# Spectra: both products copied whole out of PSUM by ScalarE, and VectorE's complex products fed from SBUF alone

## The chip, the cores and the metric

The kernel runs on one core of a Trainium2 chip. The metric is the device time of one execution in microseconds (us); smaller is better. The core's engines work side by side, each through its own queue in order: TensorE (PE, with its weight loads PEld), VectorE (DVE), ScalarE (ACT), GpSimd (POOL), and SyncE (SP), which issues most of the DMAs. TensorE writes its products into PSUM; DVE and ACT read them there; SBUF is the large memory that all engines and the DMAs share.

## The reference

Two independent layers read two inputs of 2048 rows and 576 columns, and their outputs are put side by side:

```python
qkv = (x @ wqkv) ...                          # 32 heads of 18 columns
scores = einsum("bhqd,bhkd->bhqk", q, k) * (Dh ** -0.5)
mask = (i - j >= 0) & (i - j < 256)           # sliding window
a = softmax(where(mask, scores, -1e9)) @ v, heads joined, @ wo

P = exp(dt * A * l)                           # 576 channels, 128 states, l = 0..2047
K = einsum("dn,dnl,dn->dl", C, P, dt * B).real
Kf = rfft(pad(K)); Uf = rfft(pad(u))          # length 4096
y = irfft(Uf * Kf)[:, :2048] + u * Dskip
out = concatenate([a, y])
```

The change touches only `Uf * Kf`: the spectrum of the input times the spectrum of the filter, a complex product for each frequency and channel.

## The kernel before

The work is written as some twenty streams (Python generators), each of which yields at every step. A string of letters, `PLAN`, says in which order the steps are issued: a letter alone takes the next step of a stream, a letter with a digit runs the oldest follow-up that the stream posted under that digit. So the order on every engine is written out by hand and does not depend on how long anything takes.

The part that matters is the last one (`"rest"`). There run together: `smax` (letter s; for a head group and 64 queries at a time it multiplies Q with K, line 831, adds the mask, line 839, and DVE takes the row maximum, line 865, `red`), `scores` (a; the same products once more with the maximum taken off, lines 901 and 914, then ACT takes the exponential into `P`, line 919), `pv` (v; `P` times `V`, line 939, into the PSUM tile `po`), `norm` (n; two DVE transposes, lines 964 and 968, then a POOL multiplication, line 973, an ACT copy, line 977, and a POOL subtraction, line 981), `wo` (w; the last projection) and the convolution: `cspec` (c), `cinv` (d) and `clast` (e).

`cspec` calls `spectra(n)` for 24 tiles, 3 groups of 192 channels by 8 groups of frequencies. For each tile it takes two PSUM slots `pi[0]` and `pi[1]`; a second-stage Fourier matrix is multiplied with a tile `x` that holds 192 columns of the input and 192 of the filter side by side (line 671, 32 matmuls). So `pi[0]` holds the real parts of both spectra and `pi[1]` the imaginary parts, each as 128 partitions x 2 x 384: columns 0 to 191 the input, 192 to 383 the filter. Three follow-ups form the complex product: `first` (c1, ACT, line 679), `second` (c2, DVE, line 686) and `third` (c3, POOL, lines 691 and 692).

All these products go through one PSUM pool, `ring`, of three slots; only `po` has its own. A slot can be written again when the last instruction that reads it is done, so each matmul group waits for the reader of an earlier one. `X`, `t1` and `t2` live in the pool `fy`, with one buffer each.

Of the kernel before, what the change touches and what calls it, by code (L numbers as in the profile page):

```python
# [10 lines left out]
F32 = mybir.dt.float32  # L11
# [3 lines left out]
AF = mybir.ActivationFunctionType  # L15
OP = mybir.AluOpType
# [114 lines left out]
class Kernel:  # L131
# [14 lines left out]
    def pow2_scale(self, parts, nm):  # L146
# [4 lines left out]
        r = sp.tile([128, 1], F32, name=nm + "r")  # L151
        nc.vector.tensor_reduce(m, parts, axis=AX.X, op=OP.max)
        nc.gpsimd.partition_all_reduce(g, m, 128, bass.bass_isa.ReduceOp.max)
# [508 lines left out]
    def spectra(self, n):  # L662
        nc, tt, fy, t = self.nc, self.nc.vector.tensor_tensor, self.p["fy"], n % 8
        x, pi = self.cl.pop(n), (self.slot(), self.slot())
        for i in range(2):
            for q in range(2):
                for s in range(2):
                    for r in range(2):
                        b = 2 * q + (r ^ s)
                        o = (2 * s + q) * 64 + 32 * i  # L670
                        nc.tensor.matmul(pi[i][32 * b:32 * b + 32, s, :384], self.w2[64 * r:64 * r + 64, t, o:o + 32],  # L671
                                         x[64 * r:64 * r + 64, 2 * s + q].rearrange("p m j -> p (m j)"),
                                         start=True, stop=True, skip_group_check=True)
        sh = [128, 2, 2, 192]

        def first():
            X = fy.tile(sh, F32, name="X")
            for i in range(2):
                nc.scalar.activation(X[:, :, i], pi[i][:, :, :192], AF.Copy)  # L679
            self.post("2", (X, *pi), lambda: second(X))  # L680

        def second(X):
            t1 = fy.tile(sh, F32, name="t1")
            t2 = fy.tile(sh, F32, name="t2")
            for i, tm in enumerate((t1, t2)):
                tt(tm, X, pi[i][:, :, 192:384].unsqueeze(2).to_broadcast(sh), op=OP.mult)  # L686
            self.post("3", (t1, t2), lambda: third(t1, t2))

        def third(t1, t2):
            Y = self.Y[n] = self.p["fs"].tile(sh, F32, name="Y")  # L690
            nc.gpsimd.tensor_tensor(Y[:, 0], t1[:, :, 0], t2[:, :, 1], op=OP.subtract)  # L691
            nc.gpsimd.tensor_tensor(Y[:, 1], t1[:, :, 1], t2[:, :, 0], op=OP.add)
            self.n["Y"] += 1
        self.post("1", pi, first)

    def inverse(self, n):
# [167 lines left out]
    def red(self, out, x):  # L864
        self.nc.vector.tensor_reduce(out, x, axis=AX.X, op=OP.max)  # L865
        self.n["max"] += 1
# [319 lines left out]
```

## Time and profile before

| | |
|---|---|
| time, median of 3 runs | 879.57 us (873.76 to 879.66) |
| the profiled execution's own time | 875.76 us |
| its span, first to last instruction | 874.0 us, mean granted TensorE clock 0.923 |
| busy over the span | PE 719.8, DVE 601.3, ACT 526.9, POOL 378.1 us |
| `spectra`, first and last product on DVE | start at 449.6 and 783.9 us |

An execution's time is a little longer than its span, by 1.76 us here. In the groups of instructions a row gives line, engine, operation, output and input with their shapes, the count, then the busy time with the mean of one in ns, and behind the second bar the idle time of the engine just before these instructions and what ended it. In the timeline a row gives start, duration, engine, line, operation, count, and in brackets how long the engine had been idle and who released it; rows with x2 merge two instructions that follow each other.

### The profile page before, as it was taken

The page shows a single profiled execution, that of the slowest core. Times are in us where ns is not written, and L with a number is a line of the kernel's source. Part 1 is how long each engine was busy: PE and PEld are TensorE (multiplying, and loading weights), DVE is VectorE, ACT ScalarE, POOL GpSimd, SP SyncE. Part 2 cuts the span into 40 slices and gives each one's busy share as a digit, 9 for nine tenths or more (in the row PEclk, how much of TensorE's full clock was granted, in tenths as well). Part 3 has the DMA queues.
Part 4 walks back from the last instruction along what each step waited for, and adds up shares of the span by engine and source line. Part 5 has one row for each costly group of instructions (what it writes and reads, how often), then busy time and mean ns, then how long its engine had stood idle before and what let it go on. Part 6 is the DMA issues. An engine that isn't in the chain of part 4 may idle for free. (4 is left out here: it accounts for less than half of the span.)

```text
span 874.0 us, 29447 instructions
## 1 busy us (share of the span) xinstructions
PE 719.8 (82%) x12954; PEld 417.3 (48%) x12954; DVE 601.3 (69%) x798; ACT 526.9 (60%) x709; POOL 378.1 (43%) x295
## 2 busy tenths in 40 slices
PE   3575957999889888896887779868998988989977
PEld 2331523456345644564534445435454544557655
DVE  5865887887987787776757798667787778751010
ACT  3247676578777766672455567646776776666421
POOL 2266857666687755565013424321242151432020
PEclk9985969999999999995889999969999998999998
DMA  9795261546347754569457856947658675746743
GB/s 306 263 236 138 61 162 34 143 92 164 85 103 193 151 131 135 116 158 251 102 184 237 270 182 211 215 116 243 176 156 270 192 238 159 205 128 188 244 139 123
DMA packets 211040, 150.74 MB, mean 172 GB/s; under 512 B 102698, under 2 KB 191530, under 8 KB 210656
## 3 DMA queue, kind: packets, MB, share of 16 engines
q1 hardware_dynamic: 208896, 144.87, 59.0%
q0 software_dynamic: 2016, 3.99, 1.4%
q8 instruction: 101, 1.65, 0.8%
q14 instruction: 27, 0.22, 0.1%
HBM read 83.57 MB, written 65.11 MB: 170 GB/s over the span
## 5 line engine op out<-in xcount | busy, mean ns | idle before, releaser
L865 DVE TENSOR_REDUCE m<-ring 128x2 f32<-128x640 f32 (+4 forms) x256 | 186.8, 779 | 52.8 <-PE ring L839 49.5
L919 ACT ACTIVATE P<-ring,esc 128x1024 f32<-128x1024 f32 (+2 forms) x160 | 167.5, 1060 | 85.6 <-PE ring L914 78.0
L546 POOL TENSOR_TENSOR m<-A,tr 128x1024 f32<-128x1024 f32 x72 | 144.0, 2019 | 77.8 <-DVE m L552 66.7
L939 PE MATMUL po<-P,V 64*32 64x320 f32 (+4 forms) x2816 | 101.6, 364 | 4.7 <-issue 4.7
L831 PE MATMUL ring<-K,Q 54*64 54x320 f16 (+4 forms) x1024 | 82.2, 319 | 26.8 <-DMA K<-kz 8.0
L691 POOL TENSOR_TENSOR Y<-t,t 128x384 f32<-128x384 f32 x24 | 24.0, 1002 | 138.9 <-DVE t L686 129.9
L973 POOL TENSOR_TENSOR osb<-osb,T 128x1024 f32<-128x1024 f32 x16 | 37.9, 2366 | 99.1 <-DVE T L968 61.4
L901 PE MATMUL ring<-Q,K 55*64 55x320 f16 (+4 forms) x1408 | 67.2, 269 | 14.5 <-DVE t L686 5.6
L831 PEld LDWEIGHTS <-Q 54*64 54x64 f16 x1024 | 44.2, 109 | 71.5 <-issue 64.0
L981 POOL TENSOR_TENSOR oh<-osb,oh 128x1024 f16<-128x1024 f32 x16 | 34.1, 2134 | 68.6 <-ACT oh L977 68.5
L178 PE MATMUL pp<-xh,wh 128*128 128x512 f16 x180 | 48.4, 400 | 18.6 <-ACT vst L365 9.2
L686 DVE TENSOR_TENSOR t<-X,ring 128x768 f32<-128x768 f32 x48 | 43.4, 945 | 25.5 <-ACT X L679 18.3
L178 PEld LDWEIGHTS <-wh 128*128 128x128 f16 x324 | 32.0, 102 | 57.7 <-issue 19.4
L901 PEld LDWEIGHTS <-K 55*64 55x64 f16 x1408 | 34.0, 109 | 47.5 <-issue 40.5
L552 DVE TENSOR_TENSOR m<-m,m 128x1024 f32<-128x1024 f32 x36 | 53.4, 1482 | 4.8 <-POOL m L546 4.7
L839 PE MATMUL ring<-sm,idb 64*64 64x128 bf16 x896 | 56.0, 225 | 0.1
L575 PE MATMUL ring<-Q,m 128*32 128x64 f32 x2304 | 42.6, 231 | 16.1 <-DVE m L552 13.4
L939 PEld LDWEIGHTS po<-P,V 64*32 64x32 f32 x2816 | 38.6, 107 | 34.6 <-issue 24.9
L575 PEld LDWEIGHTS ring<-Q,m 128*32 128x32 f32 x2304 | 37.0, 117 | 29.6 <-issue 11.9
L178 PE MATMUL pp<-xh,wl 128*128 128x512 f16 x180 | 50.6, 417 | 0.0
L964 DVE STREAM_TRANSPOSE T<-osb 128x1024 f32<-128x1024 f32 x16 | 19.8, 1235 | 42.1 <-ACT osb L949 42.1
L527 POOL TENSOR_TENSOR tr<-tr,mab 128x768 f32<-128x768 f32 x18 | 33.7, 1871 | 31.2 <-ACT tr L522 31.1
(159 smaller groups left out, 1539.4 us busy)
## 6 DMA issues: line engine op xcount, KB each, us to landing
gx<-ust SPq DMA_DIRECT2D x16, 576.0 KB
gk<-kst SPq DMA_DIRECT2D x18, 512.0 KB
xk<-gx SPq DMA_DIRECT2D x24, 384.0 KB
xk<-gk SPq DMA_DIRECT2D x24, 384.0 KB
h<-ho SPq DMA_DIRECT2D x48, 192.0 KB
hp<-h SPq DMA_DIRECT2D x12, 768.0 KB
Q<-qz SPq DMA_DIRECT2D x16, 512.0 KB
K<-kz SPq DMA_DIRECT2D x16, 512.0 KB
```

What stands on the lines that cost most here:

```text
L178: self.nc.tensor.matmul(ps, u, v, start=(i == 0), stop=(i == len(ops) - 1))
L546: tt(m[part], A[:, ch, a0:a0 + 8].unsqueeze(3).to_broadcast(sh), tr[:, ch, part, 0:8].unsqueeze(2).to_broadcast(sh), op=OP.mult)
L552: self.nc.vector.tensor_tensor(m[0], m[0], m[1], op=OP.add)
L575: nc.tensor.matmul(kp[32 * st:32 * st + 32, j, :], m[:, ch, 32 * term:32 * term + 32], Q[:, ch, term, :], start=(term == 0), stop=(term == ...
L686: tt(tm, X, pi[i][:, :, 192:384].unsqueeze(2).to_broadcast(sh), op=OP.mult)
L831: nc.tensor.matmul(ps[z:z + 64, b, :n], d["Q"][rr, 2 * b + pp, 64 * qb:64 * qb + 64], d["K"][rr, 2 * b + pp, k0:k1], start=True, stop=Fals ...
L839: nc.tensor.matmul(out, self.idb[rr], self.sm[rr], start=False, stop=True, skip_group_check=True)
L865: self.nc.vector.tensor_reduce(out, x, axis=AX.X, op=OP.max)
L901: nc.tensor.matmul(ps[z:z + 64, b, off:off + w], d["K"][rr, 2 * b + pp, kc:kc + 64], d["Q"][rr, 2 * b + pp, q0:q0 + w], start=(k == 0), st ...
L919: nc.scalar.activation(P[:, :, lo:hi], ps[:, :, lo:hi], AF.Exp, scale=self.esc)
L939: nc.tensor.matmul(po[32 * p:32 * p + 32, z, q0:q0 + w], V[64 * z:64 * z + 64, kb * 76 + 19 * p:kb * 76 + 19 * p + 32], P[p % 2][64 * z:64 ...
L973: nc.gpsimd.tensor_tensor(osb, osb, rb, op=OP.mult)
```

## The change

ACT now copies all 384 columns of each slot, both the input's and the filter's, so `X` doubles from 3 KB to 6 KB in each partition (its layout is now part, half of the frequencies, column). DVE's two products take both operands out of `X`, the input's part through a rearranged view so that `t1` and `t2` come out as before, and no longer read PSUM. `post("2", ...)` names only `X`.

```diff
         def first():
-            X = fy.tile(sh, F32, name="X")
+            X = fy.tile([128, 2, 2, 384], F32, name="X")
             for i in range(2):
-                nc.scalar.activation(X[:, :, i], pi[i][:, :, :192], AF.Copy)
-            self.post("2", (X, *pi), lambda: second(X))
+                nc.scalar.activation(X[:, i], pi[i][:, :, :384], AF.Copy)
+            self.post("2", (X,), lambda: second(X))
 
         def second(X):
             t1 = fy.tile(sh, F32, name="t1")
             t2 = fy.tile(sh, F32, name="t2")
             for i, tm in enumerate((t1, t2)):
-                tt(tm, X, pi[i][:, :, 192:384].unsqueeze(2).to_broadcast(sh), op=OP.mult)
+                tt(tm, X[:, :, :, :192].rearrange("p i s j -> p s i j"),
+                   X[:, i, :, 192:].unsqueeze(2).to_broadcast(sh), op=OP.mult)
             self.post("3", (t1, t2), lambda: third(t1, t2))
```

No instruction changes its place on any engine; what changes is what some of them wait for. Behind line 679 the new file has one line more, so line 901 there is 902, 914 is 915, 939 is 940 and 865 is 866 (lines up to 686 keep their numbers). The order on PE at one `spectra` tile, the sixteenth, which starts at 664 us in the trace; its second slot's matmuls come first, then two score blocks, each of which takes the next slot of `ring`. Before:

```order
L671 MATMUL ring<-xk,w_5121 32x384 [waits Activation_49]
L671 MATMUL ring<-xk,w_5121 32x384 x7
L901 LDWEIGHTS K_4393
L901 MATMUL ring<-Q_4392,K_4393 64x320 [waits DVE_49]
...
L914 MATMUL ring<-tm,idb 64x2x128
L901 LDWEIGHTS K_4393
L901 MATMUL ring<-Q_4392,K_4393 64x320 [waits DVE_49]
...
L939 MATMUL po<-P,V_4394 32x320 x8
```

And now:

```order
L671 MATMUL ring<-xk,w_5121 32x384 [waits Activation_49]
L671 MATMUL ring<-xk,w_5121 32x384 x7
L902 LDWEIGHTS K_4393
L902 MATMUL ring<-Q_4392,K_4393 64x320 [waits DVE_49]
...
L915 MATMUL ring<-tm,idb 64x2x128
L902 LDWEIGHTS K_4393
L902 MATMUL ring<-Q_4392,K_4393 64x320 [waits Activation_49]
...
L940 MATMUL po<-P,V_4394 32x320 x8
```

The first block writes the third slot, which an earlier row maximum has to release, in both. The second block writes the slot of `pi[0]`: before it waited for DVE's product, now it waits for ACT's copy. The same tile on DVE, ahead of it the end of one run of row maxima and behind it the next. Before:

```order
L865 TENSOR_REDUCE m<-ring 128x2 [waits PE_49] x10
L686 TENSOR_TENSOR t_10125<-X,ring 128x768 [waits DVE_49,Activation_49,Pool_49]
L686 TENSOR_TENSOR t_10126<-X,ring 128x768 [waits DVE_49,PE_49]
L865 TENSOR_REDUCE m<-ring 128x2 [waits PE_49] x6
L851 TENSOR_SCALAR m_10302<-ring 32x128 [waits DMAHW2_49,DMAHW1_49,DMAHW3_49,DMAHW0_49,PE_49]
```

And now:

```order
L866 TENSOR_REDUCE m<-ring 128x2 [waits PE_49] x10
L686 TENSOR_TENSOR t_10125<-X 128x768 [waits DVE_49,Activation_49,Pool_49]
L686 TENSOR_TENSOR t_10126<-X 128x768 [waits DVE_49]
L866 TENSOR_REDUCE m<-ring 128x2 [waits PE_49] x6
L852 TENSOR_SCALAR m_10302<-ring 32x128 [waits DMAHW2_49,DMAHW1_49,DMAHW3_49,DMAHW0_49,PE_49]
```

The two products stand where they stood, ahead of six row maxima; `ring` is gone from their inputs, and the second no longer waits for PE.

## Prediction

> **What bounds the kernel now.** I read the chain of work that ended last first, then the stage in which the change lies, then who waits for the changed instructions. The chain, by engine and by line:
>
> ```profile
> PE 26%; DVE 7%; DMA 5%; ACT 4%; issue 2%; SPq 1%; ACTq 0%; DVEq 0%
> PE ring L178 7%; PE po L939 5%; DVE m L865 4%; PE ring L703 3%; ACT P L919 3%; PE ring L831 3%; PE ring L901 3%; PE ring L671 2%; DVE t L686 2%; DMA V<-vd 1%; PE ring L764 1%; PE ring L914 1%; DMA oh<-od 1%; DMA hp<-h 1%; DVE T L964 1%
> ```
>
> PE leads, and between its pieces stand short visits to the engines that empty its slots: row maxima on DVE, exponentials on ACT, and the complex products at line 686 with 2%. All 24 tiles of the spectra lie between 447 and 790 us. The busy time there, in the order PE, PEld, DVE, ACT, POOL:
>
> ```profile
> 447.00:790.00 343.00, 294.61 (x7518) 163.32 (x7502) 250.79 (x327) 221.98 (x250) 109.22 (x76) 0.96 0.66 194
> ```
>
> PE is idle for 48 us of 343, DVE for 92, ACT for 121. No engine is full; what can be won is PE's 48 us, and they are short stalls. The source view of line 686 says which of them end at a product; ahead of them stands what the products themselves waited for most:
>
> ```profile
>   ACT X L679: 18.3, 10
>   PE ring L703: 6.7, 6
>   PE ring L901: 5.6, 8
>   PE ring L831: 3.0, 4
>   PE ring L764: 1.2, 2
> ```
>
> The last four sum to 16.5 us of PE idle time that a product ended by giving back a slot. Weight loads show the same stalls in rows of their own; they are not added.
>
> **Part one: what the instructions cost.** Groups of the same or the nearest form, and the spread (min/median/max) of line 552, a sum of two SBUF tiles on DVE:
>
> ```profile
> L686 DVE TENSOR_TENSOR t<-X,ring 128x768 f32<-128x768 f32 x48 | 43.4, 945 | 25.5 <-ACT X L679 18.3 <-issue 4.8 <-POOL Y L692 2.1
> L679 ACT ACTIVATE X<-ring 128x384 f32<-128x384 f32 x48 | 23.4, 490 | 10.8 <-PE ring L671 8.2 <-DVE t L686 1.1 <-ACT osb L949 0.2
> L771 ACT ACTIVATE y<-ring 128x768 f32<-128x768 f32 x12 | 9.7, 810 | 6.0 <-PE ring L764 6.0
> L263 DVE TENSOR_TENSOR rre<-nA_re,hre 96x768 f32<-96x768 f32 x1 | 1.0, 953 | 0.0
> L552 DVE TENSOR_TENSOR m<-m,m x36: 1210/1218/2972, 84.1 to 417.6; 128x1024 f32<-128x1024 f32 x36
> ```
>
> A whole copy is of the form of line 771, which reads the same 2 x 384 columns of a ring slot: 810 ns instead of 490. That is 48 x 0.32 = 15.4 us more on ACT, which rises to 237 of 343 us. A product with both operands in SBUF and POOL at rest takes 953 ns by line 263, so 48 x 8 ns = 0.4 us more on DVE: nothing. [...]
>
> **Part two: the slot comes back earlier.** The sixteenth tile, with POOL at rest:
>
> ```profile
> 664.13 1.52 PE L671 MATMUL ring<-xk,w 64*32 64x384 f32 x32
> 665.11 0.49 ACT L679 ACTIVATE X<-ring 128x384 f32<-128x384 f32 x1
> 665.76 0.49 ACT L679 ACTIVATE X<-ring 128x384 f32<-128x384 f32 x1 [0.15 <-PE ring L671]
> 666.22 1.11 ACT L919 ACTIVATE P<-ring,esc 128x1024 f32<-128x1024 f32 x1
> 666.34 1.82 DVE L686 TENSOR_TENSOR t<-X,ring 128x768 f32<-128x768 f32 x2 [1.26 <-ACT X L679]
> 667.34 0.41 PE L901 MATMUL ring<-Q,K 55*64 55x320 f16 x8 [1.24 <-DVE t L686]
> 667.97 1.11 ACT L919 ACTIVATE P<-ring,esc 128x1024 f32<-128x1024 f32 x1 [0.64 <-PE ring L914]
> 669.40 0.39 PE L901 MATMUL ring<-Q,K 55*64 55x256 f16 x8
> ```
>
> With the change the first copy ends at 665.11 + 0.81 = 665.92, and PE, ready at 667.34 - 1.24 = 666.10, goes on at once: the stall of 1.24 us is gone. But ACT now ends its second copy at 666.73 and not 666.25, its two exponentials follow each other without a gap, 666.77 to 667.88 and on to 668.99, and the second ended at 669.08 before. The score block at 669.40 takes the slot that this exponential frees, so it starts at about 669.03: of 1.24 us gained 0.37 are left, 30%. What is next late is ACT, whose added 0.64 us stands right there. I take 30% of 16.5: **4.9 us gained**. The bounds are 0 and 16.5.
>
> The products start half a microsecond later wherever DVE waits for `X` (18.3 us, 10 times; about 5 us over the stage), and the row maxima queued behind them on DVE move too, with PE waiting for those. That lies inside the 30%.
>
> **Part three: two SBUF operands and POOL.** Line 552 takes 1218 ns as a rule and up to 2972. Three neighbours show when, and three others what happens between two DVE instructions:
>
> ```profile
> 224.97 1.81 POOL L527 TENSOR_TENSOR tr<-tr,mab 128x768 f32<-128x768 f32 x1 [5.53 <-ACT tr L522]
> 225.00 2.85 DVE L552 TENSOR_TENSOR m<-m,m 128x1024 f32<-128x1024 f32 x1
> 226.86 1.50 POOL L532 TENSOR_TENSOR t<-tr,wr 128x256 f32<-128x256 f32 x1
> 81.99 4.04 POOL L546 TENSOR_TENSOR m<-A,tr 128x1024 f32<-128x1024 f32 x2
> 83.72 0.49 DVE L475 TENSOR_SCALAR fr<-fr 128x512 int32<-128x512 int32 x1
> 84.14 2.97 DVE L552 TENSOR_TENSOR m<-m,m 128x1024 f32<-128x1024 f32 x1
> ```
>
> POOL's instruction begins at 224.97 and ends at 226.78; DVE's, issued 0.03 us later, ends at 227.85, so it ran only after POOL's; and POOL's next one was held in turn until DVE had finished. They exclude each other. In the second place POOL's second instruction got in between two of DVE's: the one issued at 84.14 ended at 87.11, some 1.1 us after POOL's had ended at 86.03. Today the products escape this, as the tile at 653 us shows:
>
> ```profile
> 652.73 0.49 ACT L679 ACTIVATE X<-ring 128x384 f32<-128x384 f32 x1 [0.15 <-PE ring L671]
> 653.25 2.38 POOL L973 TENSOR_TENSOR osb<-osb,T 128x1024 f32<-128x1024 f32 x1 [12.37 <-ACT X L679]
> 653.25 1.82 DVE L686 TENSOR_TENSOR t<-X,ring 128x768 f32<-128x768 f32 x2
> 655.87 1.56 DVE L865 TENSOR_REDUCE m<-ring 128x2 f32<-128x640 f32 x2 [0.80 <-PE ring L839]
> 656.75 0.33 PE L831 MATMUL ring<-K,Q 54*64 54x320 f16 x4 [0.29 <-DVE m L865]
> ```
>
> Both products took 1.82 us beside POOL's line 973. With the change `X` is there at about 653.75, POOL has been at work since 653.25 and ends at 655.63; the products end at 657.45 instead of 655.07, 2.4 us later. The row maxima start at 657.45 and not 655.87, 1.6 us later, and PE at 656.75 waits for the first of them: a loss of about 1.55 us there. At other places nothing follows:
>
> ```profile
> 584.30 1.78 DVE L686 TENSOR_TENSOR t<-X,ring 128x768 f32<-128x768 f32 x2
> 588.31 0.28 DVE L851 TENSOR_SCALAR m<-ring 32x128 f16<-32x128 f32 x1 [2.23 <-PE ring L847]
> ```
>
> Here DVE was idle for 2.23 us behind the products, and a delay of 2.4 us shows as 0.2. Going through the timeline of POOL and DVE, 8 of the 24 pairs lie within reach of line 973 or 981; the first and the last are
>
> ```profile
> 465.74 2.36 POOL L973 TENSOR_TENSOR osb<-osb,T 128x1024 f32<-128x1024 f32 x1 [8.26 <-issue]
> 466.88 1.82 DVE L686 TENSOR_TENSOR t<-X,ring 128x768 f32<-128x768 f32 x2 [1.28 <-ACT X L679]
> 781.20 2.40 POOL L973 TENSOR_TENSOR osb<-osb,T 128x1024 f32<-128x1024 f32 x1
> 783.04 1.82 DVE L686 TENSOR_TENSOR t<-X,ring 128x768 f32<-128x768 f32 x2 [3.90 <-ACT X L679]
> ```
>
> Five of the eight are no accident: line 973 and the products are both released by the transpose of line 968, which stands just ahead of them on DVE. The price of one lies between 0 and 2.4 us; between the 0.2 and the 1.55 of the two places I take 1.0, nearer to the second, since DVE is busy for 73% of the stage: **8.0 us lost**, bounds 0 and 19.
>
> POOL's own delays (up to 0.95 us for a product ahead of it) fall on `norm`, whose results are needed tens of microseconds later: nothing.
>
> **The sum.** 875.76 - 4.9 + 8.0 = 878.9 us on the profiled execution's own time. The median of the three runs shown is 3.8 us above it, with 5.9 us between them; allowing for a third of that, I predict **880 us**: no change that can be told. About 1%, 8.8 us, is what a measurement of this kernel can tell from no change.
>
> **Rivals.** *PE keeps what it gets.* If the third slot and ACT are not next late, all 16.5 us come through: 859. For it: in every one of those stalls the copy would be done before PE arrives, and ACT is idle for a third of the stage. In some places the slots also rotate better, since the slot pair is given back at the copies, which stand earlier in the order than the products. Against: the place at 664. Chance 0.20.
>
> *The exclusion decides.* All eight pairs pay up to 2.4 us, with the row maxima behind them and PE waiting: 875.8 - 4.9 + 19.2 = 890, so it is slower by over 1%. It decides once an average conflict costs PE more than 1.7 us, that is (8.8 + 4.9) / 8. For it: the transpose releases both sides at once, and POOL can slip in between the two products, as at 84.14. Against: the idle DVE behind the products at 584. Chance 0.23. [...]
>
> *ACT's queue decides.* The added 15.4 us stand ahead of exponentials that PE waits for (3% of the chain is line 919). With all of it on the path and the 4.9 kept: 886. For it: the copies are followed by an exponential at most tiles. Against: ACT is at 69% afterwards. Chance 0.10.
>
> **Chances and range.** The forecast has 0.47, with 871 to 889 as its own range. Faster by over 1% is the first rival, 0.20; slower by over 1% the other two, 0.33; within 1% 0.47. Eight times in ten the time lies from 863 (all 16.5 kept, with the median's 3.8 us on top) to 893 (all eight conflicts at 2.4 us and the same 3.8 on top).
>
> **What would show it.** In the new profile line 679 should stand at 810 ns, ACT at 15 us more, and the PE stalls released by line 686 should be gone, with ACT's line 679 in their place at no more than 3 us. Line 686 should have a median near 950 and a maximum of 2 to 3.3 us, with a mean near 1.2 to 1.4 us; if its maximum stays near 960, part three is wrong and so is the loss. If PE's idle time in the stage falls from 48 us to under 38 the first rival is right; if the waits for line 865 grow by over 10 us, the second.

## The result, and the profile after

The changed kernel takes 886.22 us as the median of 6 runs (882.93 to 894.39), the kernel before 873.59 us in 6 runs beside them on the same chip. The ratio is 1.012, with a 95% interval of 1.0085 to 1.0156: 10.5 us slower, 7.4 to 13.7 (the two medians alone lie 12.6 us apart). The predicted 880 us and its range of 863 to 893 held the time, but the likeliest case, "no change that can be told", did not: at 1.2% the loss lies just past the 8.8 us that were called measurable, though its interval still reaches below them. That 886 lies between the 871 and 889 of that case comes of a range that stands around 880; 1% above the 873.6 us that the kernel before took here is 882. What came is the second rival, in which the exclusion of VectorE (DVE) and GpSimd (POOL) decides.

The profiled execution took 885.03 us with a span of 883.3, 9.3 us more than that of before. Some 3 us of this stood already at the first copy of a spectrum, ahead of any changed instruction (450.91 us against 447.84), so that the two profiles alone show about 6 us; the runs decide.

In the profile after, line numbers from 687 on are one higher (the row maxima are line 866, normalisation's multiplication is 974 and its subtraction 982). The source view of the changed lines (min/median/max) and the group of the products:

```profile
L679 ACT ACTIVATE X<-ring x48: 797/811/817, 450.9 to 792.5; 128x768 f32<-128x768 f32 x48
L686 DVE TENSOR_TENSOR t<-X x48: 916/956/3120, 453.0 to 794.8; 128x768 f32<-128x768 f32 x48
L686 DVE TENSOR_TENSOR t<-X 128x768 f32<-128x768 f32 x48 | 56.9, 1225 | 32.3 <-ACT X L679 24.1
```

The copies cost what was forecast, 811 ns. The products nearly keep their median (956 ns, 948 before), but their longest takes 3.1 us, and all 48 together 56.9 us instead of 43.4. The waits of PE in the stage, first of after, then the row of before that answers to the first of them:

```profile
PE ring L832 <- DVE m L866: 17.9, 22, 3.4
PE ring L832 <- ACT P L920: 4.6, 11, 0.9
```

```profile
PE ring L831 <- DVE m L865: 4.3, 17, 0.4
```

The 16.5 us in which PE waited for a product are gone from the list. The waits for row maxima grew from 4.3 to 17.9 us, the longest from 0.4 to 3.4. So PE is idle for as long as before. The windows view runs from the start of the first product to the end of the last, before and then after. Its columns are those of the prediction, and behind the five engines stands TensorE's granted clock as a share of full speed (0.96 and 0.93):

```profile
449.65:784.86 335.21, 286.95 (x7398) 158.79 (x7390) 250.79 (x327) 217.10 (x244) 105.27 (x74) 0.96 0.66 196
```

```profile
453.04:795.71 342.67, 294.18 (x7400) 163.23 (x7385) 263.44 (x327) 228.70 (x244) 109.09 (x74) 0.93 0.65 191
```

The stage is 7.5 us longer, and PE is idle in it for 48.5 us, 48.3 before. Nearly all of the 7.5 us is PE's busy time: the same matmuls took 294.2 us instead of 287.0, at a lower granted clock. This is not one execution alone: the mean granted clock of the changed kernel's six runs is 0.915, and 0.928 over the 28 runs of the kernel before that stand beside runs 5 to 8. In the trace of after the clock stands at 0.50 from 521 to 527 us and from 722 to 725, around the end of the first and just behind the second of the two waits of PE of over 3 us that the next rows show; at the same two tiles before it is 1.00. It stands at 0.50 from 558 to 563 too, around a wait of 3.10 us for a DMA (line 765), and in the kernel before from 573 to 589 with no wait over 0.8 us just ahead of it. What lowers it was not tested.

DVE gained 12.7 us of busy time with the same 327 instructions, and that is no work but waiting inside them. Two places in the timeline of after show it, the seventh and the eighteenth tile (rows between them left out):

```profile
517.31 4.00 DVE L686 TENSOR_TENSOR t<-X 128x768 f32<-128x768 f32 x2
517.47 3.02 POOL L974 TENSOR_TENSOR osb<-osb,T 128x1024 f32<-128x1024 f32 x1 [9.35 <-DVE T L969]
521.23 3.06 DVE L866 TENSOR_REDUCE m<-ring 128x2 f32<-128x640 f32 x4
522.10 0.48 PE L832 MATMUL ring<-K,Q 54*64 54x320 f16 x4 [3.44 <-DVE m L866]
...
713.55 2.37 POOL L974 TENSOR_TENSOR osb<-osb,T 128x1024 f32<-128x1024 f32 x1 [1.75 <-DVE T L969]
714.00 5.54 DVE L686 TENSOR_TENSOR t<-X 128x768 f32<-128x768 f32 x2 [0.59 <-ACT X L679]
715.92 2.79 POOL L982 TENSOR_TENSOR oh<-osb,oh 128x1024 f16<-128x1024 f32 x1
719.46 0.81 DVE L866 TENSOR_REDUCE m<-ring 128x2 f32<-128x640 f32 x1
720.32 0.33 PE L832 MATMUL ring<-K,Q 54*64 54x320 f16 x4 [3.34 <-DVE m L866]
```

At 517 the first product is issued before line 974, so line 974 (2.36 us alone) waits 0.66 us for it; then the second product waits for line 974. The pair, 1.83 us long when POOL rests, ends 4.00 us after its start, the row maxima start late, and PE waits 3.44 us. At 714 the order is POOL, product, POOL, product: line 974, then one product, then line 982, which was issued while the first product was waiting or at work and is 2.79 us long instead of 2.13, then the second product. 5.54 us for the pair, and PE waits 3.34 us.

Pairs above 2 us stand at seven tiles, numbers 3, 7, 12, 15, 17, 18 and 24 in order, seven of the eight that the prediction had counted. The eighth, number 5, held POOL instead (line 982 took 2.89 us there). The seven add some 13 us to the products.

### The profile page after: what moved, and what is told of

Same layout as the page of the kernel before. It is cut to its first block, busy times and chain, and to the rows that moved or that the text cites. A ratio compares the mean times of both kernels' runs of the same rounds, so it can differ in the third digit from the quotient of the medians.

```text
span 883.3 us, 29450 instructions
## 1 busy us (share of the span) xinstructions
PE 725.9 (82%) x12954; PEld 421.3 (48%) x12954; DVE 613.0 (69%) x798; ACT 538.8 (61%) x709; POOL 381.8 (43%) x295
## 4 chain that ended last, share of the span: by engine, by line
PE 46%; DVE 20%; ACT 12%; DMA 9%; issue 8%; POOL 3%; SPq 3%; ACTq 0%; DVEq 0%; POOLq 0%
PE pp L178 10%; PE ring L178 6%; PE po L940 6%; DVE m L866 5%; PE ring L704 4%; PE ring L902 3%; DVE t L686 3%; ACT P L920 3%; PE ring L832 3%; PE ring L671 3%; PE ring L575 2%; PE ring L453 2%; PE ring L465 2%; DMA Q<-m 1%; PE ring L591 1%
## 5 line engine op out<-in xcount | busy, mean ns | idle before, releaser
L902 PE MATMUL ring<-Q,K 55*64 55x320 f16 (+4 forms) x1408 | 69.5, 276 | 12.2 <-ACT P L920 4.0
L686 DVE TENSOR_TENSOR t<-X 128x768 f32<-128x768 f32 x48 | 56.9, 1225 | 32.3 <-ACT X L679 24.1
L982 POOL TENSOR_TENSOR oh<-osb,oh 128x1024 f16<-128x1024 f32 x16 | 36.6, 2288 | 65.0 <-ACT oh L978 52.5
L178 PE MATMUL pp<-xh,wh 128*128 128x512 f16 x180 | 48.8, 403 | 17.9 <-ACT vst L365 9.2
L575 PE MATMUL ring<-Q,m 128*32 128x64 f32 x2304 | 43.2, 232 | 16.0 <-DVE m L552 13.7
```

The lines of the kernel that those rows point to most:

```text
L178: self.nc.tensor.matmul(ps, u, v, start=(i == 0), stop=(i == len(ops) - 1))
L575: nc.tensor.matmul(kp[32 * st:32 * st + 32, j, :], m[:, ch, 32 * term:32 * term + 32], Q[:, ch, term, :], start=(term == 0), stop=(term == ...
L686: tt(tm, X[:, :, :, :192].rearrange("p i s j -> p s i j"), X[:, i, :, 192:].unsqueeze(2).to_broadcast(sh), op=OP.mult)
L902: nc.tensor.matmul(ps[z:z + 64, b, off:off + w], d["K"][rr, 2 * b + pp, kc:kc + 64], d["Q"][rr, 2 * b + pp, q0:q0 + w], start=(k == 0), st ...
```

## The experiments

Each time is the ratio to the kernel before, run on the same chip between the others; 1% is 8.8 us. Where two rows are set against each other, both are taken relative to the kernel before. Theory A is that the loss is the exclusion and that the earlier slot is a gain hidden under it; theory B that ScalarE (ACT) makes it slow.

| what runs | ratio | 95% interval |
|---|---|---|
| the changed kernel | 1.0120 | 1.0085 to 1.0156 |
| 1: whole copies alone | 1.0041 | 1.0012 to 1.0069 |
| 2: SBUF products, half copies | 1.0047 | 1.0011 to 1.0083 |
| 3: changed, POOL's order rewritten at all tiles | 1.0103 | 1.0056 to 1.0149 |
| 4: before, the same order | 1.0119 | 1.0067 to 1.0170 |
| 5: before, POOL's part of the normalisation cut | 0.9973 | 0.9939 to 1.0006 |
| 6: changed, the same cut | 0.9910 | 0.9876 to 0.9945 |
| 7: SBUF products, half copies, the same cut | 0.9888 | 0.9850 to 0.9926 |
| 8: changed, POOL's order rewritten at six tiles | 1.0043 | 1.0009 to 1.0076 |
| 9: changed form at 17 tiles | 0.9993 | 0.9970 to 1.0017 |
| 10: changed form at the other seven | 1.0085 | 1.0054 to 1.0117 |
| 11: changed form at 16 tiles | 0.9934 | 0.9901 to 0.9966 |
| 12: changed form at 11 tiles | 0.9925 | 0.9890 to 0.9960 |

**1. ScalarE's longer copies alone.** Against the changed kernel:

```diff
-            self.post("2", (X,), lambda: second(X))
+            self.post("2", (X, *pi), lambda: second(X))
...
-                   X[:, i, :, 192:].unsqueeze(2).to_broadcast(sh), op=OP.mult)
+                   pi[i][:, :, 192:384].unsqueeze(2).to_broadcast(sh), op=OP.mult)
```

> ScalarE copies the ring slot whole, as in the changed kernel, but the products go on reading their second operand from PSUM, so a slot is still given back by the products and no product has two SBUF operands. Nothing is left out. What it isolates is ScalarE's added 0.32 us per copy, 48 times. Theory A (the exclusion of VectorE and POOL makes the changed kernel slow): line 679 stands at 810 ns, line 686 stays near 945 to 960 ns with a maximum under 1.1 us, the stalls of PE on line 686 stay near 17 us or rise by a few us since the products start later, and the time is within 1% of before, 0 to +5 us. Theory B (ScalarE's longer copies make it slow): slower than before by as much as the changed kernel or more, +10 to +16 us, with the waits for line 919 or 865 grown.

Measured: +3.6 us (1.1 to 6.0). The group of the products, and PE's waits for them in the stage:

```profile
L686 DVE TENSOR_TENSOR t<-X,ring 128x768 f32<-128x768 f32 x48 | 43.6, 950 | 30.3 <-ACT X L679 22.4
```

```profile
PE ring L704 <- DVE t L686: 8.2, 6, 1.8
PE ring L902 <- DVE t L686: 7.3, 7, 1.8
...
PE ring L832 <- DVE t L686: 4.6, 5, 1.6
```

As theory A had it, no product is long. But the copies are not free: the products start later (DVE waits 22.4 us for `X`, 18.3 before), and these three stalls of PE stand at 20.1 us, 15.3 before. That is about a third of the change's loss and not all of it; theory B falls as the main cause.

**2. SBUF operands and the early slot, without the longer copies.** Against the changed kernel (`flt` is a tile of ones, filled once ahead):

```diff
-            X = fy.tile([128, 2, 2, 384], F32, name="X")
+            X = fy.tile(sh, F32, name="X")
...
-                nc.scalar.activation(X[:, i], pi[i][:, :, :384], AF.Copy)
+                nc.scalar.activation(X[:, :, i], pi[i][:, :, :192], AF.Copy)
...
-                tt(tm, X[:, :, :, :192].rearrange("p i s j -> p s i j"),
-                   X[:, i, :, 192:].unsqueeze(2).to_broadcast(sh), op=OP.mult)
+                tt(tm, X, self.flt[:, i].unsqueeze(2).to_broadcast(sh), op=OP.mult)
```

> ScalarE copies only the input half of a slot, as before, and the products take that copy and a constant SBUF tile of ones in place of the filter's spectrum: the filter's spectrum is left out of the computation. The products have two SBUF operands and the slot comes back at the copies, without ScalarE's added 15 us. Theory A (exclusion): line 686 has products of 2.8 to 5.5 us for a pair as in the changed kernel, the waits for line 865 (866) grow by about 10 us or more, and the time is slower than before by 0.5 to 1.2%. Theory B (ScalarE's copies): no slower than before, -5 to 0 us or better, since the stalls on line 686 (16.5 us) are gone and nothing was added to ScalarE.

Measured: +4.1 us (1.0 to 7.3). The group and the wait that matters:

```profile
L686 DVE TENSOR_TENSOR t<-X,flt 128x768 f32<-128x768 f32 x48 | 59.5, 1279 | 22.3 <-ACT X L679 16.1
```

```profile
PE ring L833 <- DVE m L867: 18.9, 21, 3.6
```

Just under the 0.5% from which theory A's expectation ran, and slower although ACT does no more than before: the loss has a second part that ACT does not explain, and the long products and the waits for row maxima stand as in the changed kernel.

**3 and 4. Keeping POOL away by its own order.** In both kernels the sum and difference (step `c3`) is put right behind the products (`c2`), and an `n3` (line 973) up to 12 steps ahead of them behind that:

```diff
...
+    for i in two:
+        after[i] = ["c3"]
+        for k in range(i - 1, max(i - 13, 0), -1):
+            if t[k] in ("n1", "n6", "c2"):
+                break
+            if t[k] == "n3":
+                late.add(k)
+                after[i].append("n3")
+                break
...
+PLAN["rest"] = y_first(PLAN["rest"])
```

> The changed kernel with its order of work rewritten for POOL alone: the sum and difference of the products (line 692) is issued right behind the products, and a multiplication of line 973 that stood up to 12 steps ahead of those products is moved behind that. So POOL, in its own order, waits for the products and does not read SBUF beside them at the places where the transpose of line 968 releases both. Nothing is left out. Theory A (exclusion): line 686 loses most of its pairs above 2.3 us (its mean falls from 1225 to below 1.1 us), the waits for line 866 fall by 8 us or more, and the time is 6 to 14 us below the changed kernel, level with the kernel before or below it. Theory B (ScalarE): the products get shorter, but the time stays within 3 us of the changed kernel.

> The kernel before with the same rewriting of POOL's order (control). Nothing is left out. Its products read PSUM and were not held by POOL, so by theory A the time stays that of the kernel before within 3 us; if moving POOL's work is worth something (or costs something) by itself, it shows here and is to be taken off the other run. Theory B says the same of this run.

Measured: +9.0 us (4.9 to 13.1) and +10.4 us (5.9 to 14.9). Both expectations on the control were wrong: the rewriting costs as much by itself as the change does. Nor did the 6 to 14 us come that theory A had expected from it in the changed kernel. Alone, the run on the changed kernel would have looked like theory B. The control turns it round: between the two kernels in the same order no difference is left (1.0103 / 1.0119 = 0.998, 0.992 to 1.005; the interval is too wide to show the early slot's gain either). Its products are short again:

```profile
L709 DVE TENSOR_TENSOR t<-X 128x768 f32<-128x768 f32 x48 | 44.8, 974 | 30.3 <-ACT X L702 24.6
```

Why the order is dear is in the timeline of the control (lines are 23 higher there):

```profile
597.64 1.00 POOL L714 TENSOR_TENSOR Y<-t,t 128x384 f32<-128x384 f32 x1 [24.86 <-PE ring L726]
599.56 2.35 POOL L996 TENSOR_TENSOR osb<-osb,T 128x1024 f32<-128x1024 f32 x1
601.86 2.13 POOL L1004 TENSOR_TENSOR oh<-osb,oh 128x1024 f16<-128x1024 f32 x1
604.02 1.02 ACT L972 ACTIVATE osb<-po 128x1024 f32<-128x1024 f32 x1 [4.05 <-POOL oh L1004]
605.10 2.04 PE L962 MATMUL po<-P,V 64*32 64x320 f32 x48 [4.11 <-ACT osb L972]
```

POOL sat for 24.86 us until it could do the sum and difference, and the normalisation stood behind that; its buffer came free late, ACT's copy out of PSUM waited 4.05 us for it and PE 4.11 us. This is one place; the rest of the 10.4 us was not traced.

**5, 6 and 7. The exclusion taken away without touching any order.** POOL's two instructions of the normalisation read 2 of 512 columns, and a memset fills what the second leaves out:

```diff
-        nc.gpsimd.tensor_tensor(osb, osb, rb, op=OP.mult)
+        nc.gpsimd.tensor_tensor(osb[:, :, 0:2], osb[:, :, 0:2], rb[:, :, 0:2], op=OP.mult)
...
-            nc.gpsimd.tensor_tensor(h[:, 1], osb, h[:, 0], op=OP.subtract)
+            nc.gpsimd.memset(h[:, 1], 0.0)
+            nc.gpsimd.tensor_tensor(h[:, 1, :, 0:2], osb[:, :, 0:2], h[:, 0, :, 0:2], op=OP.subtract)
```

> The kernel before, with POOL's two instructions of the normalisation (lines 973 and 981) cut to 2 of 512 columns: most of the normalisation is left out, and POOL hardly reads SBUF in this stage. A control for the two runs beside it: what they differ by, they differ by without POOL. All theories: 0 to 4 us below the kernel before, since results of the normalisation are ready 2 us earlier but needed much later.

> The changed kernel with the same cut of POOL's two instructions (most of the normalisation is left out). The exclusion is gone; ScalarE's longer copies and the earlier return of the slot stay. The runs so far put ScalarE's longer copies alone at +0.4% and the products from SBUF alone at +0.5%. Theory A (the loss from SBUF operands is the exclusion, and the earlier slot is a gain hidden under it): line 686 stands at 956 ns with no pair above 2 us, and the time is within 3 us of the control, -4 to +3. Theory B (nearly all of the change's 10 us has another cause than POOL): 8 us or more above the control.

> As the run with half copies and a constant tile of ones in place of the filter's spectrum (the filter's spectrum is left out), and POOL's two instructions of the normalisation cut to 2 columns as well (most of the normalisation is left out). What is left against the control is the earlier return of the slot alone: neither the exclusion nor longer copies. Theory A: faster than the control by 3 to 10 us, that is what the early slot is worth; 4.9 us was the prediction's own term for it, 16.5 if PE kept all. If the early slot is worth nothing, the time is that of the control within 2 us, and the exclusion alone cost the 4 us that the half copies showed.

The products and the wait for row maxima, first in the changed form (run 6), then with half copies (run 7):

```profile
L686 DVE TENSOR_TENSOR t<-X 128x768 f32<-128x768 f32 x48 | 43.8, 953 | 32.0 <-ACT X L679 24.0
```

```profile
PE ring L832 <- DVE m L866: 10.2, 23, 1.4
```

```profile
L686 DVE TENSOR_TENSOR t<-X,flt 128x768 f32<-128x768 f32 x48 | 43.6, 948 | 22.9 <-ACT X L679 16.7
```

```profile
PE ring L833 <- DVE m L867: 9.3, 21, 1.5
```

With POOL out of the way all products are short. The windows view of run 6, from its first product to its last, and PE's wait behind the seventh tile, where the changed kernel had 3.44 us:

```profile
452.51:781.53 329.02, 284.26 (x7396) 157.53 (x7381) 250.34 (x327) 228.80 (x244) 65.42 (x88) 0.97 0.66 199
```

```profile
517.77 0.33 PE L832 MATMUL ring<-K,Q 54*64 54x320 f16 x4 [1.28 <-DVE m L866]
```

The stage is 13.7 us shorter than in the changed kernel: 9.9 us of it is PE's busy time for the same matmuls, at a clock of 0.97 instead of 0.93, and 3.7 us is PE's idle time. Over run 6's twelve executions the mean clock is 0.927, close to the 0.928 of the kernel before. So with POOL out of the way the lower clock is gone too. That the exclusion alone brings it is not shown: runs 3 and 8, whose products are nearly short but whose order is rewritten, have 0.917 and 0.916.

The sign turns. Against the control (run 5) the changed kernel is 5.5 us faster (0.9910 / 0.9973 = 0.9937, intervals combined as squares: 1.3 to 9.7), a little more than theory A expected; with half copies it is 7.5 us faster (0.9915; 3.0 to 11.9), within what was expected. So the early slot is worth about 7 us, ACT's longer copies take 2 to 4 us of it (3.6 in run 1; 1.9 +- 4.5 between runs 6 and 7), and the exclusion costs the rest: 1.0120 / 0.9937 = 1.018, that is 16 us (11 to 21). With half copies it costs 1.0047 / 0.9915 = 1.013, 12 us (6 to 17).

**8. POOL's order rewritten at six tiles only,** numbers 3, 7, 12, 15, 17 and 18, an `n3` up to 13 steps ahead, or else the next one behind, going with the `c3`:

```diff
...
+PLAN["rest"] = y_some(PLAN["rest"], (3, 7, 12, 15, 17, 18))
```

> The changed kernel with POOL's order rewritten at six of the 24 tiles only, those whose products were held by line 974 in its trace: there line 692 and then line 974 stand right behind the products. Nothing is left out. The rewriting at all places cost the kernel before 1.2% by itself, through late results of the normalisation; at six places it should cost little of that. Theory A: the pairs above 3 us of line 686 at these tiles are gone, its mean falls below 1.1 us, and the time is 4 to 9 us below the changed kernel, level with the kernel before within 4 us. If late results of the normalisation cost as much as the exclusion at these six places too, it stays within 3 us of the changed kernel.

Measured: +3.8 us (0.8 to 6.7), 6.7 us below the changed kernel by the ratios (2 to 11). The products are nearly short, and the price of the last runs is seen at one place:

```profile
L709 DVE TENSOR_TENSOR t<-X 128x768 f32<-128x768 f32 x48 | 46.5, 1010 | 29.6 <-ACT X L702 21.7
```

```profile
PE po L963 <- ACT osb L973: 4.1, 1, 4.1
```

Theory A held: with the same instructions on every engine, and POOL's order changed at six tiles, about two thirds of the loss are gone.

**9 and 10. The form chosen tile by tile.** Now POOL's order stays, and the seven tiles with long pairs get the form of before (run 9), or they alone the changed form (run 10, the complement of the set); counted from 0:

```diff
+HELD = {2, 6, 11, 14, 16, 17, 23}
...
+            w = 192 if n in HELD else 384
             for i in range(2):
-                nc.scalar.activation(X[:, i], pi[i][:, :, :384], AF.Copy)
-            self.post("2", (X,), lambda: second(X))
+                nc.scalar.activation(X[:, i, :, :w], pi[i][:, :, :w], AF.Copy)
+            self.post("2", (X, *pi) if n in HELD else (X,), lambda: second(X))
...
-                   X[:, i, :, 192:].unsqueeze(2).to_broadcast(sh), op=OP.mult)
+                   (pi[i][:, :, 192:384] if n in HELD else X[:, i, :, 192:]).unsqueeze(2).to_broadcast(sh), op=OP.mult)
```

> The changed form at 17 of the 24 tiles, the form of before at the seven tiles whose products were held by POOL in the changed kernel's trace (numbers 3, 7, 12, 15, 17, 18 and 24 in order): there ScalarE copies the input half and the products read PSUM. POOL's order is untouched and nothing is left out. Theory A (loss by exclusion at these tiles 13 to 16 us, gain by the early slot 5 to 8 us over all tiles, ScalarE's copies 2 to 4 us): line 686 (691 here) has no pair above 2.4 us, and the time is 1 to 5 us below the kernel before, that is below both kernels. If the exclusion finds other tiles as the order in time shifts, pairs above 3 us appear at other tiles and the time lies between the two kernels.

> The complement: the changed form at those seven tiles alone, the form of before at the 17 others. Nothing is left out. Theory A: the loss sits in these seven tiles, about 2 us each; with 7 of 24 parts of the early slot's gain (2 us) and of ScalarE's copies (1 us) against it the time is 9 to 14 us above the kernel before, as slow as the changed kernel or slower, though only 14 of 48 products are changed. If the loss is spread over all tiles (ScalarE's queue, later products), it is 7/24 of the changed kernel's 10 us, about 3 us.

Measured: -0.6 us (-2.6 to +1.5) and +7.4 us (4.7 to 10.2). The two groups of products of run 10:

```profile
L690 DVE TENSOR_TENSOR t<-X,ring 128x768 f32<-128x768 f32 x34 | 30.8, 947 | 19.7 <-ACT X L683 13.4 <-issue 4.1 <-POOL Y L697 2.1
L690 DVE TENSOR_TENSOR t<-X 128x768 f32<-128x768 f32 x14 | 22.0, 1612 | 8.9 <-ACT X L683 8.8
```

The loss sits in the seven tiles: 14 of 48 products changed, and the kernel is slower by 7.4 us, not by the 3 us of an even spread, though less than the 9 expected. Run 9 fell short of its 1 to 5 us. In its timeline the fifth tile had taken the place of the others:

```profile
482.91 3.71 DVE L690 TENSOR_TENSOR t<-X 128x768 f32<-128x768 f32 x2
483.49 2.33 POOL L986 TENSOR_TENSOR oh<-osb,oh 128x1024 f16<-128x1024 f32 x1 [1.17 <-ACT oh L982]
485.78 3.06 POOL L978 TENSOR_TENSOR osb<-osb,T 128x1024 f32<-128x1024 f32 x1
```

**11 and 12. Without the fifth tile; and only where PE had waited.** Each against run 9:

```diff
-HELD = {2, 6, 11, 14, 16, 17, 23}
+HELD = {2, 4, 6, 11, 14, 16, 17, 23}
```

```diff
-HELD = {2, 6, 11, 14, 16, 17, 23}
+HELD = set(range(24)) - {5, 7, 8, 9, 13, 15, 18, 19, 20, 21, 22}
```

> As the run with the changed form at 17 tiles, with the fifth tile put back to the form of before too: in that run's trace its pair of products had taken 3.71 us beside POOL's lines 986 and 978, the one pair above 2 us that was left. Nothing is left out. Theory A: no pair above 2.4 us is left unless the order in time shifts again, and the time is 1 to 3 us below the run with 17 tiles, 1 to 5 us below the kernel before. If the early slot's gain sits at the tiles that were put back (their stalls in the kernel before sum to 5.6 of 16.5 us), or is eaten by ScalarE's longer copies, it stays level with the kernel before within 1.5 us.

> The changed form only at the eleven tiles that had a stall of PE of 0.39 us or more released by line 686 in the kernel before and stand clear of POOL's lines 973 and 981 (numbers 6, 8, 9, 10, 14, 16, 19, 20, 21, 22 and 23 in order; their stalls sum to 10.3 us); the form of before at the 13 others, which saves 13 of 24 tiles ScalarE's longer copies. Nothing is left out. Theory A: no long pairs, stalls on line 686 down to about 6 us, and the time 2 to 5 us below the kernel before, at or below the run with 16 tiles. If stalls removed are given back at the next late engine, as at the sixteenth tile, 30% of 10.3 is 3 us, less 1 us for ScalarE's copies.

Measured: -5.8 us (-8.7 to -3.0) and -6.6 us (-9.6 to -3.5). The two cannot be told apart; both are faster than the kernel before and than the changed one, and by a little more than was expected. The products of run 11, and PE's wait for row maxima, then the products of run 12:

```profile
L690 DVE TENSOR_TENSOR t<-X 128x768 f32<-128x768 f32 x32 | 29.2, 954 | 21.4 <-ACT X L683 13.5 <-issue 5.8 <-POOL Y L697 2.1
L690 DVE TENSOR_TENSOR t<-X,ring 128x768 f32<-128x768 f32 x16 | 14.4, 940 | 5.3 <-ACT X L683 5.2
```

```profile
PE ring L836 <- DVE m L870: 6.5, 16, 1.3
```

```profile
L690 DVE TENSOR_TENSOR t<-X,ring 128x768 f32<-128x768 f32 x26 | 23.6, 947 | 18.9 <-ACT X L683 14.9 <-POOL Y L697 2.1 <-issue 1.6
L690 DVE TENSOR_TENSOR t<-X 128x768 f32<-128x768 f32 x22 | 20.1, 954 | 11.4 <-ACT X L683 7.3 <-issue 4.1
```

One tile put back, the fifth, brought 5.2 us between runs 9 and 11 where 1 to 3 were expected; the two were not run side by side, and their intervals leave room for 2 to 9. That PSUM operands alone make the difference is best seen at the twelfth tile, first in run 11 and then in the changed kernel, POOL's multiplication issued 0.22 us behind the products in both:

```profile
583.57 1.78 DVE L690 TENSOR_TENSOR t<-X,ring 128x768 f32<-128x768 f32 x2
583.79 2.36 POOL L978 TENSOR_TENSOR osb<-osb,T 128x1024 f32<-128x1024 f32 x1 [17.08 <-DVE T L973]
```

```profile
595.86 3.95 DVE L686 TENSOR_TENSOR t<-X 128x768 f32<-128x768 f32 x2
596.08 2.92 POOL L974 TENSOR_TENSOR osb<-osb,T 128x1024 f32<-128x1024 f32 x1 [16.46 <-DVE T L969]
```

## Why the prediction was right in its range and wrong in its case

**Part one, the cost of the instructions.** The durations held: 811 ns for a copy, 953 ns for a product beside a resting POOL (run 6), 945 before. Where the operands lie hardly showed in them: 43.8 us for 48 products from SBUF (run 6) against 43.4 with one operand in PSUM (before). What was missed is the path: the sum charged nothing of ACT's 15.4 us beyond the 30%, and alone they cost 3.6 us (run 1): the products waited 22.4 us for `X` instead of 18.3 and gave their slots back later, and PE's three stalls on them stand at 20.1 us instead of 15.3.

**Part two, the slot.** Right in mechanism and near in size. The stalls by line 686 went, and line 679 did not come in their place as a releaser (one wait of 0.5 us, of a weight load). The early slot is worth 7.5 us alone and 5.5 together with ACT's copies (runs 7 and 6), where 4.9 had been taken; the 30% fits, 5.5 of 16.5 being 33%, but it had been read at a single tile, and 1.3 to 9.7 us leave room for 8 to 59%. The first rival (all 16.5 us kept) falls: even with POOL away PE had 10.2 us of waits for row maxima where it had 4.3, so that DVE's queue and not only ACT is next late.

**Part three, the exclusion, is the term that was mis-sized.** The mechanism, the lines and the tiles were right: seven of the eight pairs counted were held. The price was not. 1.0 us per conflict and 8.0 in all had been taken "between the 0.2 and the 1.55 of the two places"; the runs give 16 us (11 to 21), 2.0 us for each of eight (1.4 to 2.7), where the second rival decides from 1.7. Two places had been priced in the trace of before, those at 653 and 584; they are the fifteenth and twelfth tile, and in the changed kernel PE waits there for what stands behind the products on DVE:

```profile
667.85 0.33 PE L832 MATMUL ring<-K,Q 54*64 54x320 f16 x4 [1.75 <-DVE m L866]
...
600.06 0.41 PE L902 MATMUL ring<-Q,K 55*64 55x192 f16 x8 [0.93 <-DVE m L852]
```

1.75 us where 1.55 had been worked out on top of the 0.29 that stood there, and 0.93 where 0.2 had been. The other five stand at 1.61, 3.44, 1.01, 3.34 and none. The seven sum to 12.1 us, but with POOL out of the way (run 6) 1.28 of them stand at the seventh tile and 0.40 at the fifteenth all the same. So the exclusion's part is about 10.4 us, 1.5 for each. The prediction took the loss as what one POOL instruction adds to a pair less DVE's idle time behind it. At 517 the pair was held for 2.17 us and PE waits 2.16 us longer than in run 6, so that nothing of the delay was hidden there. And at 714 a second POOL instruction (line 982) followed the first, which "up to 2.4 us" does not hold: PE waits 3.34 us.

These waits alone would leave the average below the 1.7 us. What the sum had no term for is the granted clock, 0.93 in the stage where it had been 0.96, and 0.97 with POOL away. The prediction looked for gain and loss in PE's idle time, which did not move; its busy time did.

"POOL's own delays fall on `norm` ...: nothing" held for the 0.95 us that it was said of: no wait of PE in the changed kernel names a copy of `osb`. It does not hold for longer ones (runs 4 and 8: 4.1 us in one piece).

**The sum.** -5.5 + 16 is +10.5, where -4.9 + 8.0 = +3.1 had stood. It closes because the 16 was worked out as the rest, and so is no test of its own. That the predicted 880 came 1.1 us nearer to the 886 than the sum's 878.9 is luck: the added third of 3.8 us lay on the same side. "The waits for line 865 grow by over 10 us" was the second rival's mark, and they grew by 13.6; 5.9 of that stand in run 6 as well.

## What to carry to other kernels

Before an operand is moved from PSUM to SBUF for VectorE, look at what GpSimd does at that moment: here, with both operands in SBUF, a product and a GpSimd instruction ran one after the other (a pair took 4.00 us at 517 and 3.95 at 596 instead of 1.83), and it showed in the row of the products as a longer maximum (3120 ns, 955 before) beside a nearly unchanged median (956 ns, 948 before). The cure need not be all or nothing: the change was worth its gain at the tiles where PE had waited and GpSimd was elsewhere, and the same edit at 11 or 16 of 24 tiles turned 1.2% slower into 0.7% faster. An idle time that does not change is no sign that nothing was lost: here PE was busy for 7.2 us more with the same matmuls, and the granted clock beside the busy time, 0.93 instead of 0.96, shows it. And an experiment that moves an order needs its control in the kernel before, or its own cost is read as that of the cause.

## What was not expected of the hardware

That the two engines took turns instruction by instruction, and at 714 twice around one pair; the prediction had seen at 84.14 only that POOL can slip in once. Two products issued back to back were no block: in the pairs at 517, 596 and 714 an instruction of POOL that was waiting went first when one product ended, and the second product waited for all of it. A pair took 1.83 us beside a resting POOL, about 4.0 with one such instruction between its products and 5.54 with one ahead and one between. POOL paid too: 2.79 us at 714 for an instruction of 2.13, and 2.92 to 3.06 at 596, at 517 and, in run 9, at 486 for one of 2.36. With one operand in PSUM neither paid: at 583 in run 11 the pair took 1.78 us beside POOL's 2.36.

What stays open is the exact price: 16 us (11 to 21) by runs 5 and 6, about 10.4 us by the seven waits of PE in the changed kernel's trace, and 7.4 us net in run 10. The lower granted clock fits the gap between the first two, but no run separates it from the waits. In run 10 the eighteenth pair took 2.03 us and not 5.54, which explains 3.5 us at most, and the seven tiles kept their share of the early slot's gain, which was not measured by itself.
